# Decay attention and a squared-ReLU FFN in fp32 on one core: weight sums stored sum by sum, visits that wait for one chunk per half, two early weight differences, and a last product in two halves

## The chip, the cores and the metric

One core of one Trainium2 chip runs the whole program. The metric is device time in microseconds (us) of that core, the median of several executions. Lower is better. Besides these timed executions there is one profiled execution, and all rows of the trace are from it.

## What is computed

For 4 batches of 8 heads (768 tokens, head size 64) the first stage is a linear attention with decay in blocks of 64 tokens. The second stage multiplies the attention's result, 3072 tokens of 512 features, by two weight matrices:

```python
intra = np.einsum('bhic,bhjc->bhij', qb, kb) * Dmask[None]
intra = np.einsum('bhij,bhjd->bhid', intra, vb)
inter = np.einsum('bhid,bhde->bhie', qb * lam_pow[None], kv_state)
out[:, :, sl] = intra + inter
kv_state = lam_block * kv_state + einsum('bhsd,bhse->bhde', kb * rev_pow, vb)   # shortened
...
h = np.maximum(x @ w_in, 0.0)        # 3072 x 512 by 512 x 2048
return (h * h @ w_out)               # 3072 x 2048 by 2048 x 512
```

All data are fp32. The kernel keeps that precision with three TensorE passes per product: each factor is split into a rounded part (fp32r) and the rest, and the products high by high, low by high and high by low are added in PSUM.

## The kernel before, in words

The 24 chunks of 128 tokens go through the FFN in three plain tiles (3, 3 and 2 chunks), and then in two twins of 8 chunks each. In the twins a matrix product of 2 by 2 blocks is made with seven block products instead of eight (`first_products`, `second_products`). For that, seven weight sums per pair of weight columns are made by `differences` (lines 789 to 831): three are plain quarters of the split weights, copied to DRAM, and four are differences, each made by VectorE (L824), rounded by ScalarE (L827), given its low part by VectorE (L828) and stored (L800). The whole weights that these start from are rebuilt by two additions on VectorE (L816) into a pair of `ob` buffers. There are 16 calls: `i` is 0 for the first matrix and 1 for the second, and `j` is 0 to 7. The sums lie in two DRAM tensors `kept`:

```python
kept = [tc.dram_tile([NF // 2, P, 2, 7, 2 * P], F32, name=f"kept{i}") for i in range(2)]   # line 362
```

The axes are the pair j, the partition, the part (high or low), the sum and 256 columns, so that one sum of one partition is two runs of 1 KB. In the twins each block product loads its sum back (`streamed`, L863, 256 KB into one of six buffers `b`); 224 such loads are made, one for each product of 6 matmuls in either matrix.

The attention of the later chunks is done in *visits* (`visit`, lines 678 to 719), which are put between steps of the FFN: two old chunks get their results in two halves, and two new chunks have their scores opened behind either half. The visits have two score buffers in the scratch area `work` (`s19`, 1024 words from 1024 on), which also held the weights' raw words (`st`) while the weights were prepared; `worked` (line 1169) lists the operations after which that area is free. In most visits a few FFN steps stand between the halves (`PARTED`).

The order of every engine's instructions is made when the program is built, by a list planner (`Plan.order`, lines 99 to 202). It gives every operation a duration and a key; of those that can start soon, the smallest key goes first. TensorE's order is mostly tied by hand (`link`, `linked`); the order on ScalarE, VectorE and SyncE (SP, which issues the DMAs) follows the keys and the planner's times. Buffers that share addresses are listed in `REGIONS`, with an era in `ERAS`: users of a later era wait in the plan for all users of an earlier one (`follow`). On the chip each engine runs its list in order and waits where the data need it. Calls to `differences` have the keys 470 + 30 j for the first four of the first matrix (line 1090), and wait for step 9 of the second tile and for the first tile's outputs, which use the same `ob` buffers.

At the end, `after(3)` (line 1006) adds the last product's two banks to `a6` by two VectorE additions of 128x512 (L976), and SP stores each (L982). The last product is one planned operation of six matmuls: three into the first bank, then three into the second (lines 959 to 967).

Of the kernel before, what the change touches and what calls it, by code (L numbers as in the profile page):

```python
# [62 lines left out]
class Plan:  # L63
# [176 lines left out]
PARTS = 8  # L240
D2 = 4
SPARE_FROM, SPARE_KEY = 16, 0.0
AT_ONCE = [1, 2, 4, 6, 5, 7, 3]
# [6 lines left out]
    "gh": (9216, 768), "gl": (9984, 768), "gh2": (9216, 512), "gl2": (9728, 512), "xk0": (10240, 512), "xk1": (10752, 512),  # L250
    "ob": (11264, 1024), "x": (DYN + 4672, 4096), "x2": (DYN + 4672, 2048), "xb": (DYN + 8784, 3072),
    "part": (DYN + 6720, 2048), "pt": (DYN + 6720, 4096), "pz": (DYN + 10816, 2048), "pa": (DYN + 12864, 4096), "ps": (DYN + 16960, 4096), "b": (DYN + 28288, 3072)}
# [10 lines left out]
REGIONS["ob9"] = (DYN + 4096, 512)  # L263
ERAS = {"part": 2, "x2": 2, "gh2": 2, "gl2": 2, "pa": 3, "pz": 3, "ps": 3, "pt": 3, "xk0": 3, "xk1": 3, "b": 4, "u": 4}
ERAS.update({k: 4 for k in REGIONS if k[0] == "h" and k != "hold" or k in ("xk2", "xk3", "xk4", "xk5") or k[:3] == "end"})

# [22 lines left out]
def kernel(ctx: ExitStack, tc: tile.TileContext, ka, qv, lamx, w, out):  # L289
# [43 lines left out]
    tiles["st"], tiles["m"] = [a.bitcast(U64) for a in cut(0, 1024, "st")], cut(3072, DM, "m")  # L333
    tiles["qv9"] = [a.rearrange("p (a n i) -> p a n i", a=2, n=NP) for a in cut(0, 1024, "qv9")]
    tiles["s19"] = [a.rearrange("p (n i) -> p n i", n=NP) for a in cut(1024, 256, "s19")]
    tiles["hold9"] = [a.rearrange("p (n d) -> p n d", n=NP) for a in cut(2048, 256, "hold9")]
# [341 lines left out]
    def visit(old, new, key, ahead, parted, narrow):  # L678


        heads = [range(NP)] if new else [range(n, n + 2) for n in range(0, NP, 2)]
        banks = [[Buf("bank") for _ in heads] for _ in old]

        uses, deps, chain, dots = [], [], [], []
# [104 lines left out]
    def differences(i, j, key):  # L789

        f0, f1 = 2 * j, 2 * j + 1
        raws, gate, (w0, w1), kind = [Buf("ob"), Buf("ob")], [steps[1, 9][0]] + finished[0], (ws[f0][i], ws[f1][i]), "part" if 8 * i + j < PARTS else "u"
        names = [f"{('wi', 'wo')[i]}{f}" for f in (f0, f1)]
# [4 lines left out]

        def store(c, n, get, deps, bufs, uses):
            stored[i, j].append(plan.op("SP", LOAD, 520 + 12 * j if uses and i else key, lambda: nc.sync.dma_start(  # L800
                out=kept[i][j][:, :, c:c + n].rearrange("p t c k -> p t (c k)"), in_=get().bitcast(F32)), deps, bufs, lat=2.9, uses=uses))
            stored[i, j][-1].kb *= n

        if i == 0:
            store(0, 2, lambda: flat[0], w0[:2], [], names[:1])
            store(6, 1, lambda: flat[1][:, :, 2 * P:], w1[:2], [], names[1:])
        else:
            store(0, 1, lambda: flat[0][:, :, 0:2 * P], w0[:2], [], names[:1])
            store(1, 1, lambda: flat[1][:, :, 0:2 * P], w1[:2], [], names[1:])
            store(6, 1, lambda: flat[1][:, :, 2 * P:], w1[:2], [], names[1:])  # L810
        prev = []
# [11 lines left out]
        for c, (out_, a, b) in zip((2, 4, 5, 3), ((0, 2, 0), (2, 3, 2), (3, 3, 0), (1, 1, 3))):  # L823
            o = plan.op("DVE", tt(256), key, lambda out_=out_, a=a, b=b: nc.vector.tensor_tensor(out=side(out_), in0=side(a), in1=side(b), op=ALU.subtract), prev, raws)  # L824
            part = Buf(kind)
            pair = lambda part=part: at(part) if kind == "part" else rounded[part.slot].rearrange("p (t k) -> p t k", t=2)
            oh = plan.op("ACT", act(256), key, lambda pair=pair, out_=out_: nc.scalar.copy(pair()[:, 0], side(out_)), [o], raws + [part])  # L827
            ol = plan.op("DVE", tt(256), key, lambda pair=pair, out_=out_: nc.vector.tensor_tensor(  # L828
                out=pair()[:, 1], in0=side(out_), in1=pair()[:, 0], op=ALU.subtract), [oh], raws + [part])
            store(c, 1, pair, [oh, ol], [part], ())  # L830
            prev = [o]
# [28 lines left out]
    def streamed(i, j, k, key):  # L860

        b = Buf("b")
        return b, in_turn("streamed", plan.op("SP", LOAD, key - 12, lambda: nc.sync.dma_start(out=at(b).bitcast(F32), in_=kept[i][j][:, :, KEPT[k]]), stored[i, j], [b], lat=3.2))  # L863

# [51 lines left out]
    def second_products(p, start):  # L916
# [37 lines left out]
        def product(i, j, key):  # L954
# [3 lines left out]

            def fn():
                for d, bank in enumerate((d0, d1)):  # L960
                    ds = slice(d * P, d * P + P)
# [4 lines left out]
            before = {6: "r1", 7: "r2"}.get(i)  # L966
            o = link(plan.op("PE", A_PROD, key, fn, [o, oh, ol] + (st[before] if before else []), [b, hi, lo, d0, d1], mode="F", entries=12))
            products.append(o)
            last[i] = o
            sums_of(i, j)  # L970

        def copies(i, dst):
            return [plan.op("ACT", act(WIDE) + 0.09, ended(i), lambda a=a, b=b: nc.scalar.copy(at(a), at(b)), [last[i]], [a, b], uses=names) for a, b in zip(dst, banks[i])]

        def plus(i, dst, src, deps):
            return [plan.op("DVE", tt(WIDE) + 0.1, ended(i), lambda a=a, b=b, c=c: nc.vector.tensor_tensor(out=at(a), in0=at(b), in1=at(c), op=ALU.add), [last[i], o] + more, [a, b, c], uses=names)  # L976
                    for a, b, c, o, more in zip(dst, banks[i], src, *deps)]

# [5 lines left out]
        def after(i):  # L984
# [14 lines left out]
            if i == 7:  # L999
# [5 lines left out]
                store(1, 1, st["a7"], plus(5, st["a7"], st["a7"], (st["r3"], [[o] for o in o4])))  # L1005
            if i == 3:
                store(0, 1, st["a6"], plus(3, st["a6"], st["a6"], (st["u"], none)))

        return product, after
# [67 lines left out]
    for v, ((ti, f, ahead), chain) in enumerate(zip(VISITS, visits)):  # L1077
# [8 lines left out]
        later_[-1].after.append(chain[-1])  # L1086

    for i in range(2):
# [78 lines left out]
    for o in idle + [o for ch in later[:2] for o in ch.o_vd]:  # L1167
        o.after.append(ws[IDLE][1][1])
    worked = [o for f in range(NF) for o in ws[f][0][:2] + ws[f][1][:2]]
    for o in [visits[1][0]] + outs + relus[:1]:  # L1170
# [59 lines left out]
```

## Time and profile before

| | us |
|---|---|
| timed, median of 3 | 566.16 (564.36 to 566.63) |
| the profiled execution | 562.63 |
| its span, first to last instruction | 560.9 |
| TensorE matmul busy | 550.9 (98%) |
| TensorE weight loads busy | 468.3 (83%) |
| VectorE busy | 440.5 (79%) |
| ScalarE busy | 338.8 (60%) |
| queue of all planned DMAs | 136.34 MB, 76.7% of 16 engines' span |

Busy time of an engine is the union of its instructions; matmuls overlap, so that a gap is seen only where nothing runs at all. "DMA share" is the mean busy share of the core's 16 DMA engines. A DMA's landing is counted from its issue by SP to the end of its last packet. The granted TensorE clock is 1.00 in the whole span.

### The profile page before, as it was taken

What the parts mean: (1) busy time and instruction counts of PE and PEld (TensorE: products, weight loads), DVE (VectorE), ACT (ScalarE), POOL (GpSimd) and SP (SyncE); (2) the same over time, 40 slices, a digit from 0 to 9 for tenths busy, and PEclk for the clock granted to TensorE, in tenths of its full rate; (3) what the DMA queues carried; (4) which work ended last, traced back from release to release, by engine and by line L of the source; (5) the groups of instructions that cost most, each with busy time, mean ns of one, the idle gap of its engine ahead of it and who ended that gap; (6) DMA issues with size and microseconds to landing.
All of it is one profiled execution on the core that took longest, in us unless ns stands there. A gap on an engine that the chain in (4) does not pass through costs nothing.

```text
span 560.9 us, 12877 instructions
## 1 busy us (share of the span) xinstructions
PE 550.9 (98%) x4907; PEld 468.3 (83%) x4907; DVE 440.5 (79%) x866; ACT 338.8 (60%) x695; POOL 5.2 (1%) x10
## 2 busy tenths in 40 slices
PE   8999999999999999999999999999999999999997
PEld 6789899999889888877778888888888888888885
DVE  5999999894999998978877699999722224999664
ACT  5866677674544565466857766565356667763551
POOL 3000000000000000000000000000000000000000
PEclk9999999999999999999999999999999999999999
DMA  8999788873779687599998846777877666667765
GB/s 309 370 293 355 252 263 292 261 255 112 262 268 314 189 273 262 180 302 335 311 343 300 280 135 187 202 220 198 259 237 197 192 193 195 193 194 222 204 193 182
DMA packets 104685, 137.17 MB, mean 245 GB/s; under 512 B 7088, under 2 KB 89008, under 8 KB 104624
## 3 DMA queue, kind: packets, MB, share of 16 engines
q1 hardware_dynamic: 104480, 136.34, 76.7%
q8 instruction: 39, 0.64, 0.5%
q14 instruction: 22, 0.18, 0.1%
q10 hardware_dynamic: 144, 0.01, 0.0%
HBM read 100.67 MB, written 35.65 MB: 243 GB/s over the span
## 4 chain that ended last, share of the span: by engine, by line
PE 95%; DMA 3%; issue 0%; DVE 0%; SPq 0%; ACT 0%
PE bank L482 62%; PE bank L752 16%; PE bank L758 5%; PE bank L761 5%; PE bank L759 5%; DMA b<-kept 2%; DMA ka<-ka 1%; PE bank L736 1%; PE bank L731 1%; DVE end L976 0%; SPq L508 0%; PE bank L401 0%; PE bank L418 0%; DVE h L888 0%; ACT u L884 0%
## 5 line engine op out<-in xcount | busy, mean ns | idle before, releaser
L482 PE MATMUL bank<-v,b 128*128 128x512 f32 x672 | 153.4, 389 | 0.0
L482 PEld LDWEIGHTS bank<-v,b 128*128 128x128 f32 x672 | 126.0, 188 | 26.3
L935 ACT CAST v<-h 128x512 fp32r<-128x512 f32 x112 | 67.5, 621 | 57.9 <-PE bank L482 34.6
L888 DVE TENSOR_TENSOR h<-bank,u 128x512 f32<-128x512 f32 x64 | 44.2, 691 | 62.4 <-ACT u L884 32.7
L936 DVE TENSOR_TENSOR v<-h,v 128x512 fp32r<-128x512 f32 x112 | 75.2, 689 | 19.0 <-ACT v L935 9.9
L889 ACT ACTIVATE h<-h 128x512 f32<-128x512 f32 x64 | 40.2, 631 | 22.7 <-DVE h L888 19.7
L482 PE MATMUL bank<-pa,b 128*128 128x512 f32 x192 | 48.8, 390 | 1.1 <-DMA b<-kept 1.1
L758 PE MATMUL bank<-wo,gh 128*128 128x512 f32 x125 | 49.4, 395 | 0.0
L482 PE MATMUL bank<-ps,b 128*128 128x512 f32 x192 | 49.0, 391 | 0.0
L759 PE MATMUL bank<-wo,gh 128*128 128x512 f32 x125 | 49.0, 392 | 0.0
L482 PE MATMUL bank<-pt,b 128*128 128x512 f32 x192 | 46.9, 392 | 0.9 <-DMA b<-kept 0.9
L884 ACT COPY u<-bank 128x512 f32<-128x512 f32 x48 | 28.0, 582 | 30.3 <-PE bank L482 30.1
L482 PEld LDWEIGHTS bank<-pa,b 128*128 128x128 f32 x192 | 35.9, 188 | 9.0 <-DMA b<-kept 1.6
L482 PEld LDWEIGHTS bank<-pt,b 128*128 128x128 f32 x192 | 35.7, 188 | 9.1 <-issue 1.3
L943 DVE TENSOR_TENSOR h<-h,h 128x512 f32<-128x512 f32 x64 | 42.9, 685 | 0.1
L482 PEld LDWEIGHTS bank<-ps,b 128*128 128x128 f32 x192 | 35.9, 188 | 8.0 <-DVE h L888 0.5
L890 ACT ACTIVATE h<-h 128x512 f32<-128x512 f32 x64 | 38.6, 625 | 0.3
L752 PE MATMUL bank<-xb,wi 128*128 128x384 f32 x192 | 35.2, 336 | 0.0
L752 PEld LDWEIGHTS bank<-xb,wi 128*128 128x128 f32 x192 | 33.6, 188 | 0.9
L752 PE MATMUL bank<-xa,wi 128*128 128x384 f32 x180 | 34.0, 338 | 0.0
L752 PEld LDWEIGHTS bank<-xa,wi 128*128 128x128 f32 x180 | 31.6, 188 | 1.4 <-DVE work L456 0.2
L482 PE MATMUL bank<-qv,ka 64*64 64x64 f32 (+2 forms) x1040 | 26.4, 225 | 1.6 <-DMA qv<-qv 0.5
(147 smaller groups left out, 866.5 us busy)
## 6 DMA issues: line engine op xcount, KB each, us to landing
b<-kept SPq DMA_DIRECT2D x224, 256.0 KB, 3.4
work<-w SPq DMA_DIRECT2D x32, 512.0 KB, 5.3
ka<-ka SPq DMA_DIRECT2D x23, 512.0 KB, 5.5
qv<-qv SPq DMA_DIRECT2D x19, 512.0 KB, 5.6
kept<-part SPq DMA_DIRECT2D x32, 256.0 KB, 3.7
kept<-v SPq DMA_DIRECT2D x32, 256.0 KB, 5.0
kept<-wo SPq DMA_DIRECT2D x24, 256.0 KB, 4.5
kept<-wi SPq DMA_DIRECT2D x8, 512.0 KB, 4.9
```

The costliest lines, as they stand in the source:

```text
L482: nc.tensor.matmul(*args, **kw, skip_group_check=True)
L752: nc.tensor.matmul(at(h)[:, 0:n], wt[:, cc, :], xt[:, cc, :], start=k == 0, stop=k == 3 * NCC - 1)
L758: nc.tensor.matmul(at(os_[j]), at(gh)[:, sl], woh[f], start=f == 0 and ti >= SINGLE, stop=False)
L759: nc.tensor.matmul(at(os_[j]), at(gh)[:, sl], wol[f], start=False, stop=False)
L761: nc.tensor.matmul(at(os_[j]), at(gl)[:, sl], woh[f], start=False, stop=f == NF - 1)
L884: return plan.op("ACT", act(WIDE) + 0.09, key - 6, lambda: nc.scalar.copy(at(dst), at(banks[k])), [o], [banks[k], dst])
L888: o = plan.op("DVE", tt(WIDE) + 0.1, key - 6, lambda: nc.vector.tensor_tensor(out=at(b), in0=at(banks[k]), in1=at(a), op=ALU.add), deps, [ ...
L889: o1 = plan.op("ACT", act(WIDE) + 0.12, key, lambda: nc.scalar.activation(at(b), at(b), AF.Relu), [o], [b])
L890: o1 = plan.op("ACT", act(WIDE) + 0.12, key, lambda: nc.scalar.activation(at(b), at(b), AF.Square), [o1], [b])
L935: oh = plan.op("ACT", act(WIDE) + 0.12, key - 12, lambda: nc.scalar.copy(rounded[hi.slot], at(b)), made[t, 2 * j + e], [b, hi], after)
L936: ol = plan.op("DVE", tt(WIDE) + 0.1, key - 12, lambda: nc.vector.tensor_tensor(out=rounded[lo.slot], in0=at(b), in1=rounded[hi.slot], op= ...
L943: made[o] = [plan.op("DVE", tt(WIDE) + 0.1, when, lambda: nc.vector.tensor_tensor(out=at(h[o]), in0=at(h[a]), in1=at(h[b]), op=op), deps + ...
```

## The change

- The axes of `kept` are reordered: pair, sum, partition, part, columns. One sum of one partition is then one run of 2 KB, and a whole sum is one block of 256 KB. Stores of two plain quarters of the first matrix that were one DMA of 512 KB are two of 256 KB.
- In a visit with two halves, the first half is planned to wait for the first new chunk's loads only, and the second half for the second chunk's.
- The differences of j = 0 and 1 of the first matrix use two buffers `rs` over the score buffers `s19`, with keys 440 and 450, as soon as `worked` is done; `s19` becomes a later era. `gl0` is listed as a region of its own.
- The last product of the last twin is two planned operations, one per bank. Its second bank is added in two halves of 256 columns; the very last store is issued from ScalarE's queue.

```diff
-    "qv9": 1, "s19": 4, "hold9": 4, "xr9": 1, "raw9": 1, "ob9": 1,
+    "qv9": 1, "rs": 2, "s19": 4, "hold9": 4, "xr9": 1, "raw9": 1, "ob9": 1,
...
+N_RS, RS_KEY = 2, 440
...
-    "ob": (11264, 1024), "x": (DYN + 4672, 4096), "x2": ...
+    "ob": (11264, 1024), "x": (DYN + 4672, 3104), "gl0": (DYN + 7808, 768), "x2": ...
...
+REGIONS["rs"] = REGIONS["s19"] = (DYN + 1024, 1024)
+ERAS = {"s19": 2, "part": 2, ...
...
-    kept = [tc.dram_tile([NF // 2, P, 2, 7, 2 * P], F32, name=f"kept{i}") for i in range(2)]
+    kept = [tc.dram_tile([NF // 2, 7, P, 2, 2 * P], F32, name=f"kept{i}") for i in range(2)]
...
-        for ch in new:
-            deps += [ch.o_ka[1], ch.o_qv[1]] + ch.o_vd
+        loaded_ = [[ch.o_ka[1], ch.o_qv[1]] + ch.o_vd for ch in new]
+        if parted is None:
+            deps += sum(loaded_, [])
+        elif new:
+            deps += loaded_[0]
+            more = loaded_[1]
...
-            halves(1, k, dots[k])
+            halves(1, k, dots[k] + more)
...
+        kind = "rs" if i == 0 and j < N_RS else "ob"
-        raws, gate, ... = [Buf("ob"), Buf("ob")], [steps[1, 9][0]] + finished[0], ...
+        raws, gate, ... = [Buf(kind), Buf(kind)], worked if kind == "rs" else [steps[1, 9][0]] + finished[0], ...
...
-        if i == 0:
-            store(0, 2, lambda: flat[0], w0[:2], [], names[:1])
-            store(6, 1, lambda: flat[1][:, :, 2 * P:], w1[:2], [], names[1:])
-        else:
...
+        for c, k, h in ((0, 0, 0), (1, i, 1 - i), (6, 1, 1)):
+            store(c, lambda k=k, h=h: flat[k][:, :, h * 2 * P:(h + 1) * 2 * P], (w0, w1)[k][:2], [], names[k:k + 1])
...
-  ... in_=kept[i][j][:, :, KEPT[k]]), stored[i, j], [b], lat=3.2))
+  ... in_=kept[i][j][KEPT[k]]), stored[i, j], [b], lat=3.2))
...
+            if (p, i, j) == (TWINS - 1, LAST_ORDER[-1], NF // 2 - 1):
+                last[i] = [link(plan.op("PE", A_PROD / 2, key, lambda d=d, bank=bank: fn([(d, bank)]), deps, [b, hi, lo, bank], mode="F", entries=6)) for d, bank in enumerate((d0, d1))]
+                return
...
-            if i == 3:
+            if i == 3 and p < TWINS - 1:
                 store(0, 1, st["a6"], plus(3, st["a6"], st["a6"], (st["u"], none)))
+            elif i == 3:
+                for k, (a, b, done, o) in enumerate(zip(st["a6"], banks[3], last[3], st["u"])):
+                    n = N_PLAIN + 8 * p + 2 + k
+                    for q in range(k + 1):
+                        c = slice(0, WIDE) if not k else slice(q * 2 * C, q * 2 * C + 2 * C)
+                        o1 = plan.op("DVE", ..., in0=at(b)[:, c], in1=at(a)[:, c], op=ALU.add), [done, o], [a, b], uses=names)
+                        eng = ("SP", nc.sync) if k + q < 2 else ("ACT", nc.scalar)
+                        plan.op(eng[0], 1.0, start, lambda ...: eng[1].dma_start(out=out[n][:, c], in_=at(a)[:, c]), [o1], [a], uses=names)
...
-            differences(i, j, (470 + 30 * j if j < 4 else begin[2] + D2 * (j - 3)) if i == 0 else 614 + 8 * j)
+            differences(i, j, RS_KEY + 10 * j if i == 0 and j < N_RS else (470 + 30 * j if j < 4 else begin[2] + D2 * (j - 3)) if i == 0 else 614 + 8 * j)
```

## Rows read from the trace of the kernel before

**Rows 1.** Three stretches of the span: length, busy time by engine, clock, DMA share, GB/s.
```profile
34.00:231.00 197.00, 196.51 (x2307) 176.95 (x2306) 179.32 (x388) 118.99 (x262) 0.00 (x0) 1.00 0.78 258
231.00:312.00 81.00, 77.99 (x795) 63.22 (x795) 65.03 (x139) 54.38 (x114) 0.00 (x0) 1.00 0.94 307
312.00:556.00 244.00, 244.00 (x1416) 202.08 (x1415) 167.50 (x279) 142.65 (x253) 0.00 (x0) 1.00 0.71 204
```

**Rows 2.** TensorE's timeline, 214 to 295 us: its matmuls behind an idle stretch.
```profile
220.79 0.34 PE L482 MATMUL bank<-qv,ka 64*64 64x64 f32 x8 [0.49 <-issue]
...
262.41 1.62 PE L482 MATMUL bank<-pt,b 128*128 128x512 f32 x6 [0.88 <-DMA b<-kept]
...
276.06 1.66 PE L482 MATMUL bank<-pa,b 128*128 128x512 f32 x6 [1.14 <-DMA b<-kept]
...
292.37 0.35 PE L482 MATMUL bank<-work,ka 64*64 64x64 f32 x9 [0.95 <-issue]
```

**Rows 3.** DMA issues of the whole span: transfers, KB each, median us to landing.
```profile
b<-kept SPq DMA_DIRECT2D x224, 256.0 KB, 3.4
...
kept<-wi SPq DMA_DIRECT2D x8, 512.0 KB, 4.9
...
ob<-lamx ACTq DMA_DIRECT2D x1, 10.0 KB, 3.8
```

**Rows 4.** Packets, MB and share of the DMA queue, 12 to 34 us.
```profile
q1 hardware_dynamic: 2081, 7.55, 93.5%
```

**Rows 5.** The same queue, 320 to 550 us.
```profile
q1 hardware_dynamic: 46205, 45.92, 70.1%
```

**Rows 6.** The same queue and its issues, 236 to 312 us.
```profile
q1 hardware_dynamic: 21395, 23.84, 95.7%
...
b<-kept SPq DMA_DIRECT2D x46, 256.0 KB, 5.0
kept<-v SPq DMA_DIRECT2D x31, 256.0 KB, 5.0
```

**Rows 7.** Chain that ended last, 215 to 300 us: the two waits for loads.
```profile
254.76 7.51 DMA b<-kept
...
272.05 3.98 DMA b<-kept
```

**Rows 8.** SP's queue, 230 to 300 us: start, length, what, how many issues.
```profile
253.90 0.47 SPq L508 DMA_DIRECT2D work<-qv  x1
...
267.41 4.54 SPq L800 DMA_DIRECT2D kept<-v  x6
```

**Rows 9.** SP's issue time (ns, min/median/max) of 512 KB loads, 10 to 34 us.
```profile
L508 SPq DMA_DIRECT2D qv<-qv x6: 328/328/1340, 9.8 to 31.0; - x6
```

**Rows 10.** The same for the loads of sums, 240 to 312 us.
```profile
L863 SPq DMA_DIRECT2D b<-kept x43: 517/562/1257, 240.7 to 310.7; - x43
```

**Rows 11.** One stretch, columns as in the first group.
```profile
128.00:144.00 16.00, 16.00 (x198) 14.19 (x197) 8.63 (x20) 5.51 (x12) 0.00 (x0) 1.00 0.45 153
```

**Rows 12.** Groups of instructions of the whole span: busy us, mean ns of one.
```profile
L824 DVE TENSOR_TENSOR ob<-ob,ob 128x256 f32<-128x256 f32 x40 | 16.8, 420 | 0.4
...
L828 DVE TENSOR_TENSOR part<-ob,part 128x256 fp32r<-128x256 f32 x32 | 13.1, 417 | 0.2
L827 ACT CAST part<-ob 128x256 fp32r<-128x256 f32 x32 | 12.7, 404 | 16.2 <-DVE ob L824 15.8
...
L816 DVE TENSOR_TENSOR ob<-wi 128x512 f32<-128x512 f32 x16 | 10.5, 683 | 0.6 <-DMA out<-ob 0.6
```

**Rows 13.** VectorE's timeline at 152 to 155 us: the first mask into a score buffer.
```profile
153.38 0.41 DVE L568 TENSOR_TENSOR work<-bank,mask 128x256 f32<-128x256 f32 x1
```

**Rows 14.** VectorE's timeline at the end.
```profile
556.40 1.37 DVE L976 TENSOR_TENSOR end<-bank,end 128x512 f32<-128x512 f32 x2 [2.53 <-PE bank L482]
```

**Rows 15.** The last stores, 556 to 561 us, in SP's queue.
```profile
L982 SPq DMA_DIRECT2D out<-end x2: 332/332/332, 557.1 to 557.8; - x2
...
DMA to landing us min/median/max: 2.1/2.1/2.1
```

More of the change, by code (lines that the diff above doesn't have):

```diff
@@ L250 @@
     "gh": (9216, 768), "gl": (9984, 768), "gh2": (9216, 512), "gl2": (9728, 512), "xk0": (10240, 512), "xk1": (10752, 512),
[L251 removed]
+    "ob": (11264, 1024), "x": (DYN + 4672, 3104), "gl0": (DYN + 7808, 768), "x2": (DYN + 4672, 2048), "xb": (DYN + 8784, 3072),
     "part": (DYN + 6720, 2048), "pt": (DYN + 6720, 4096), "pz": (DYN + 10816, 2048), "pa": (DYN + 12864, 4096), "ps": (DYN + 16960, 4096), "b": (DYN + 28288, 3072)}
@@ L263 @@
 REGIONS["ob9"] = (DYN + 4096, 512)
-ERAS = {"part": 2, "x2": 2, "gh2": 2, "gl2": 2, "pa": 3, "pz": 3, "ps": 3, "pt": 3, "xk0": 3, "xk1": 3, "b": 4, "u": 4}
+REGIONS["rs"] = REGIONS["s19"] = (DYN + 1024, 1024)
+ERAS = {"s19": 2, "part": 2, "x2": 2, "gh2": 2, "gl2": 2, "pa": 3, "pz": 3, "ps": 3, "pt": 3, "xk0": 3, "xk1": 3, "b": 4, "u": 4}
 ERAS.update({k: 4 for k in REGIONS if k[0] == "h" and k != "hold" or k in ("xk2", "xk3", "xk4", "xk5") or k[:3] == "end"})
@@ L334 @@
     tiles["qv9"] = [a.rearrange("p (a n i) -> p a n i", a=2, n=NP) for a in cut(0, 1024, "qv9")]
+    tiles["rs"] = cut(1024, DM, "rs")
     tiles["s19"] = [a.rearrange("p (n i) -> p n i", n=NP) for a in cut(1024, 256, "s19")]
@@ L682, in visit @@
         banks = [[Buf("bank") for _ in heads] for _ in old]
-        uses, deps, chain, dots = [], [], [], []
+        uses, deps, chain, dots, more = [], [], [], [], []
         for ch in old:
@@ L791, in differences @@
         f0, f1 = 2 * j, 2 * j + 1
-        raws, gate, (w0, w1), kind = [Buf("ob"), Buf("ob")], [steps[1, 9][0]] + finished[0], (ws[f0][i], ws[f1][i]), "part" if 8 * i + j < PARTS else "u"
+        kind = "rs" if i == 0 and j < N_RS else "ob"
+        raws, gate, (w0, w1), kind = [Buf(kind), Buf(kind)], worked if kind == "rs" else [steps[1, 9][0]] + finished[0], (ws[f0][i], ws[f1][i]), "part" if 8 * i + j < PARTS else "u"
         names = [f"{('wi', 'wo')[i]}{f}" for f in (f0, f1)]
@@ L797, in differences, with store @@
         stored[i, j] = []
-        def store(c, n, get, deps, bufs, uses):
+        def store(c, get, deps, bufs, uses):
             stored[i, j].append(plan.op("SP", LOAD, 520 + 12 * j if uses and i else key, lambda: nc.sync.dma_start(
-                out=kept[i][j][:, :, c:c + n].rearrange("p t c k -> p t (c k)"), in_=get().bitcast(F32)), deps, bufs, lat=2.9, uses=uses))
-            stored[i, j][-1].kb *= n
-        if i == 0:
-            store(0, 2, lambda: flat[0], w0[:2], [], names[:1])
-            store(6, 1, lambda: flat[1][:, :, 2 * P:], w1[:2], [], names[1:])
-        else:
-            store(0, 1, lambda: flat[0][:, :, 0:2 * P], w0[:2], [], names[:1])
-            store(1, 1, lambda: flat[1][:, :, 0:2 * P], w1[:2], [], names[1:])
-            store(6, 1, lambda: flat[1][:, :, 2 * P:], w1[:2], [], names[1:])
+                out=kept[i][j][c], in_=get().bitcast(F32)), deps, bufs, lat=2.9, uses=uses))
+        for c, k, h in ((0, 0, 0), (1, i, 1 - i), (6, 1, 1)):
+            store(c, lambda k=k, h=h: flat[k][:, :, h * 2 * P:(h + 1) * 2 * P], (w0, w1)[k][:2], [], names[k:k + 1])
         prev = []
@@ L829, in differences @@
                 out=pair()[:, 1], in0=side(out_), in1=pair()[:, 0], op=ALU.subtract), [oh], raws + [part])
-            store(c, 1, pair, [oh, ol], [part], ())
+            store(c, pair, [oh, ol], [part], ())
             prev = [o]
@@ L862, in streamed @@
         b = Buf("b")
-        return b, in_turn("streamed", plan.op("SP", LOAD, key - 12, lambda: nc.sync.dma_start(out=at(b).bitcast(F32), in_=kept[i][j][:, :, KEPT[k]]), stored[i, j], [b], lat=3.2))
+        return b, in_turn("streamed", plan.op("SP", LOAD, key - 12, lambda: nc.sync.dma_start(out=at(b).bitcast(F32), in_=kept[i][j][KEPT[k]]), stored[i, j], [b], lat=3.2))
     def first_products(p, j, key):
@@ L957, in product, with fn @@
             first, end_ = i not in (6, 7) and j == 0, j == NF // 2 - 1
-            def fn():
-                for d, bank in enumerate((d0, d1)):
+            def fn(half_=((0, d0), (1, d1))):
+                for d, bank in half_:
                     ds = slice(d * P, d * P + P)
@@ L966, in product @@
             before = {6: "r1", 7: "r2"}.get(i)
-            o = link(plan.op("PE", A_PROD, key, fn, [o, oh, ol] + (st[before] if before else []), [b, hi, lo, d0, d1], mode="F", entries=12))
+            deps = [o, oh, ol] + (st[before] if before else [])
+            if (p, i, j) == (TWINS - 1, LAST_ORDER[-1], NF // 2 - 1):
+                last[i] = [link(plan.op("PE", A_PROD / 2, key, lambda d=d, bank=bank: fn([(d, bank)]), deps, [b, hi, lo, bank], mode="F", entries=6)) for d, bank in enumerate((d0, d1))]
+                return
+            o = link(plan.op("PE", A_PROD, key, fn, deps, [b, hi, lo, d0, d1], mode="F", entries=12))
             products.append(o)
-            last[i] = o
+            last[i] = [o, o]
             sums_of(i, j)
         def copies(i, dst):
-            return [plan.op("ACT", act(WIDE) + 0.09, ended(i), lambda a=a, b=b: nc.scalar.copy(at(a), at(b)), [last[i]], [a, b], uses=names) for a, b in zip(dst, banks[i])]
+            return [plan.op("ACT", act(WIDE) + 0.09, ended(i), lambda a=a, b=b: nc.scalar.copy(at(a), at(b)), [o], [a, b], uses=names) for a, b, o in zip(dst, banks[i], last[i])]
         def plus(i, dst, src, deps):
-            return [plan.op("DVE", tt(WIDE) + 0.1, ended(i), lambda a=a, b=b, c=c: nc.vector.tensor_tensor(out=at(a), in0=at(b), in1=at(c), op=ALU.add), [last[i], o] + more, [a, b, c], uses=names)
-                    for a, b, c, o, more in zip(dst, banks[i], src, *deps)]
+            return [plan.op("DVE", tt(WIDE) + 0.1, ended(i), lambda a=a, b=b, c=c: nc.vector.tensor_tensor(out=at(a), in0=at(b), in1=at(c), op=ALU.add), [done, o] + more, [a, b, c], uses=names)
+                    for a, b, c, done, o, more in zip(dst, banks[i], src, last[i], *deps)]
         def store(t, d, src, os_):
@@ L1005, in after @@
                 store(1, 1, st["a7"], plus(5, st["a7"], st["a7"], (st["r3"], [[o] for o in o4])))
-            if i == 3:
+            if i == 3 and p < TWINS - 1:
                 store(0, 1, st["a6"], plus(3, st["a6"], st["a6"], (st["u"], none)))
+            elif i == 3:
[3 more added lines that the diff above has]
+                        c = slice(0, WIDE) if not k else slice(q * 2 * C, q * 2 * C + 2 * C)
+                        o1 = plan.op("DVE", tt(WIDE / (k + 1)) + 0.1, ended(3), lambda a=a, b=b, c=c: nc.vector.tensor_tensor(out=at(a)[:, c], in0=at(b)[:, c], in1=at(a)[:, c], op=ALU.add), [done, o], [a, b], uses=names)
+                        eng = ("SP", nc.sync) if k + q < 2 else ("ACT", nc.scalar)
+                        plan.op(eng[0], 1.0, start, lambda a=a, n=n, c=c, eng=eng: eng[1].dma_start(out=out[n][:, c], in_=at(a)[:, c]), [o1], [a], uses=names)
         return product, after
@@ L1086 @@
         later_[-1].after.append(chain[-1])
+    worked = [o for f in range(NF) for o in ws[f][0][:2] + ws[f][1][:2]]
     for i in range(2):
         for j in range(NF // 2):
-            differences(i, j, (470 + 30 * j if j < 4 else begin[2] + D2 * (j - 3)) if i == 0 else 614 + 8 * j)
+            differences(i, j, RS_KEY + 10 * j if i == 0 and j < N_RS else (470 + 30 * j if j < 4 else begin[2] + D2 * (j - 3)) if i == 0 else 614 + 8 * j)
     end = [steps[2, 0][0]]
@@ L1168 @@
         o.after.append(ws[IDLE][1][1])
-    worked = [o for f in range(NF) for o in ws[f][0][:2] + ws[f][1][:2]]
     for o in [visits[1][0]] + outs + relus[:1]:
```

## The prediction

> **What bounds the kernel now.** I read the busy time by stretch first, then TensorE's idle gaps, then the chain of waits, and only then the DMA queue, because a gap says which of the other views matters. By the stretches TensorE is the bound: it works all of 312 to 556 us and all but 0.49 us of 34 to 231, at the full granted clock, and loses 3.0 us in 231 to 312, the first half of the first twin [rows 1]. Nothing that only makes another engine faster can help outside the gaps. The gaps are four: 0.49 and 0.95 us in the middle of two visits, ended by nothing that the trace shows, and 0.88 and 1.14 us before block products that waited for their weight sum [rows 2]. To these comes the tail: the last two additions start at 556.40, the last store is issued at 557.80 and the span ends at 560.9 [rows 14, 15]. So about 3.5 us of gaps and a tail of some 4.5 us are all that can be won; 550.9 us of matmuls stay.
>
> The chain names the two loads of sums: one took 7.51 us from issue to use, the other 3.98 us [rows 7], where the median of all 224 is 3.4 [rows 3]. In the stretch around them the DMA queue is full: 95.7% of 16 engines, and the median landing of a sum is 5.0 us [rows 6]. Later, at 70.1%, the same loads never stop TensorE [rows 1, 5]. The first late load stands right behind the last of three 512 KB loads of a visit, issued from 252.7 on [rows 8]. The second stands behind six stores that held SP for 4.54 us [rows 8].
>
> **The change part by part.** *Layout.* A sum is now moved in 128 runs of 2 KB, not 256 of 1 KB. No row has 2 KB packets alone, so I draw a line through two stretches. From 320 to 550 us a packet took 0.701 x 16 x 230 / 46205 = 55.8 ns at 994 B [rows 5]; from 12 to 34 us it took 0.935 x 16 x 22 / 2081 = 158 ns at 3628 B [rows 4]. That is 17 ns plus 0.039 ns per byte (an estimate from these two rows): 57 ns for 1 KB, 97 ns for 2 KB. A 256 KB sum costs 256 x 57 / 16 = 0.91 us of all engines before and 128 x 97 / 16 = 0.77 after, 15% less. From 236 to 312 us there are 46 loads and 31 stores of that kind [rows 6], so 77 x 0.14 = 10.7 us fall out of 0.957 x 76 = 72.7 us of engine time. That is the upper end; the lower is nothing, if in a full queue bytes and not packets set the pace, for the bytes stay.
>
> What each gap gets of it: the first late load needs 0.88 us of its 7.51. At this stretch's pace (315 / 0.957 = 329 GB/s [rows 6]) 7.51 us are 2.5 MB, of which 1.6 MB are the three big loads, which don't change. The remaining 0.9 MB are about 3.5 sums, 0.5 us; the backlog from before is smaller too. I take 0.7 (bounds 0 to 0.88). The second late load is late by SP. An issue takes 0.33 us with 128 runs [rows 9] and 0.52 to 0.56 with 256 [rows 10], so six stores are done 6 x 0.2 = 1.2 us sooner, unless VectorE then makes SP wait for the data. I take 1.0 (bounds 0 to 1.14). The visit's gap at 292 us lies in the full queue as well; if it is a fetch delayed by other transfers, it shrinks. I take 0.4 (bounds 0 to 0.95). The 0.49 at 220 us I leave.
>
> The Trainium skill ("DMA: Bandwidth & Descriptors", section "Why small descriptors are slow (HBM only)") gives a packet a fixed overhead of three 32-byte beats. By that alone 70 beats would become 67, an estimate of 4% instead of 15%, or 3 us instead of 10.7. The two stretches contradict it: their overhead is 17 ns where a beat of 32 B takes 1.2.
>
> The price: 8 stores of 512 KB with 2 KB runs [rows 3] become 16 stores of 256 KB whose source has 1 KB runs. That is 8 x (512 x 57 - 256 x 97) / 16 = 2.2 us more engine time and 8 x 0.52 = 4 us of SP, between 34 and 130 us. TensorE never waits for DMA or SP there [rows 1, 2], so it costs nothing; without that cover one late weight load would cost at most its own 0.52.
>
> *Visits.* Only the plan's belief changes: on the chip the first half never waited for the second chunk, and no visit from 140 us on waits for a load [rows 2]. Worth 0 itself; any new order it causes is priced below.
>
> *Early differences.* Two calls leave the crowded stretch. Each is 2 x 0.68 + 4 x 0.42 + 4 x 0.42 = 4.7 us of VectorE and 4 x 0.40 = 1.6 of ScalarE [rows 12], so 9.5 us of VectorE go forward. Between 128 and 144 us VectorE has 16 - 8.6 = 7.4 us idle [rows 11]; the missing 2 us come out of steps in which TensorE never stopped although other such calls stood between them. The score buffers are first written at 153.4 us [rows 13], 24 us after the buffers come free. So 0, on either side; without cover up to 2 us once. Relief of VectorE after 144 us is worth 0 too, as TensorE has only 0.49 us to give back there. The eight stores leave SP's queue sooner, long before the first twin. `gl0` as its own region adds no instruction: 0.
>
> *Last product.* The first bank is complete three matmuls earlier, 3 x 0.227 = 0.68 us, while VectorE has idled 2.5 us [rows 14]. So its addition runs from 555.7 to 556.4, and the two quarter-size ones from there to about 557.2 (0.42 each, 0.34 apart when back to back). The last store is issued 0.6 us sooner and moves half the bytes, up to 0.4 us less; its landing is 2.1 us now [rows 15]. I take 0.8. The bounds are 1.0 gained and 1.1 lost: the only DMA from ScalarE's queue landed after 3.8 us [rows 3], 1.7 more than a store here, of which 0.6 are given back.
>
> *Sum.* 0.7 + 1.0 + 0.4 + 0.8 = 2.9 us, out of the profiled execution's 562.63 (span 560.9 and 1.7 around it): 559.7. The timed median is 566.16, 3.5 us above the profiled execution. These 3.5 us cannot come from matmuls at a full clock; stretches that wait for DMA can vary, so more of the same stalls is the likeliest place. Bounds are none and all of it; I let a third (1.2) go with the stalls: 566.16 - 2.9 - 1.2 = 562.1 us.
>
> **The rivals.** *A, forecast:* the full queue gets room and the stalls mostly go: 562.1, own range 558.8 to 564.5. *B, bytes bind:* in the full stretch packets queue for memory, and fewer of them take as long. For it: the stretch moves 315 GB/s at 95.7% [rows 6], not far from 7.55 MB / 22 us = 343 GB/s of the big packets at 93.5% [rows 4]. Against it: that is still 9% more, at a lower share. Then the first gap loses 0.3 us, the second 0.6 by SP's shorter issues, the tail 0.8: 566.16 - 1.7 = 564.5. The Trainium skill (same page, section "Specifications") names about 358 GB/s as the memory's limit for one core, which would leave 8% over the stretch's 329 GB/s at full share; no run here shows the limit. *C, the layout doesn't do what it says:* the transfers stay cut into 1 KB runs. Against it: the 512 KB loads issue in 0.33 us [rows 9], as one run per partition would, though their tiles have several axes. Only the tail is won: 565.4. *D, slower:* the plan is made anew with times shifted by 9.5 us of VectorE, and SP's order from 231 to 312 us comes out worse: loads of sums behind runs of stores that wait for VectorE, as at 267 us. Each such place costs about 1.14 [rows 2]; there are eight rows of seven products. Beyond four such places it eats the gain; with six in place of the two of now, and no relief by the layout, it is 6 x 1.14 - 2.0 - 0.8 = +4.0: 570.2. For it: SP is in order and already has one such place. Against it: shorter issues make each cheaper.
>
> **How the numbers follow.** About 0.5% (2.8 us) can be told from no change: faster is under 563.3, slower over 569.0. A has 0.53 (faster 0.43, same 0.10), B 0.25 (0.08 and 0.17), C 0.05 (same), D 0.17 (slower 0.11, same 0.05, faster 0.01). Together: faster 0.52, same 0.37, slower 0.11. The range runs from nearly all stalls gone with most of the 3.5 us (558.5) to B, C and a mild D (567.0); the bad half of D and an end below A's are left out.
>
> **What would show it.** Packets of the queue from 104,480 to about 70,000. SP's issue of a sum near 0.33 us, landing from 236 to 312 us under 4.5, DMA share there near 0.85. No `b<-kept` wait over 0.4 us before a matmul. Stores of `part` starting near 135 us. The last store issued some 0.8 us after the last matmul, instead of 1.2. Wrong would be: a DMA share still over 0.93 with fewer packets (B), the same packets (C), or new gaps before products behind runs of stores (D).

## The result, and the profile after

The changed kernel takes 559.92 us (median of four executions, 558.94 to 560.71) against 565.38 us before on the same chip: the ratio is 0.9902, 95% interval [0.9873, 0.9931]. In a second series it was 0.9888 [0.9855, 0.9922]. The forecast was 562.1 with a range of 558.5 to 567.0, so the time fell inside, and the gain was 5.5 us where 4.1 had been forecast. The changed kernel's profiled execution took 560.71 us, with a span of 559.0.

TensorE's busy time by stretch, the same columns as in [rows 1]:

```profile
34.00:231.00 197.00, 197.00 (x2311) 177.69 (x2310) 180.56 (x390) 119.84 (x264) 0.00 (x0) 1.00 0.77 259
231.00:312.00 81.00, 78.30 (x798) 63.41 (x797) 63.93 (x137) 55.80 (x116) 0.00 (x0) 1.00 0.93 316
312.00:554.00 242.00, 242.00 (x1406) 200.46 (x1405) 166.98 (x279) 140.74 (x249) 0.00 (x0) 1.00 0.69 202
```

The 0.49 us of 34 to 231 are gone, but 231 to 312 still loses 2.7 us, and the DMA share there is still 0.93. TensorE's idle stretches behind 200 us, to be laid beside [rows 2]:

```profile
260.89 1.63 PE L485 MATMUL bank<-pt,b 128*128 128x512 f32 x6 [1.16 <-DMA b<-kept]
...
274.48 1.66 PE L485 MATMUL bank<-pa,b 128*128 128x512 f32 x6 [1.08 <-DMA b<-kept]
...
298.94 1.61 PE L485 MATMUL bank<-pa,b 128*128 128x512 f32 x6 [0.41 <-DMA b<-kept]
```

Both gaps inside visits are gone. Both waits for a sum are still there, in the same places, and a third has come. Had I stopped at this pair of profiles, I would have said that the layout did nothing for the waits; the experiments show why one pair is too little. The DMA queue and its issues from 236 to 312 us, for [rows 6]:

```profile
q1 hardware_dynamic: 12340, 24.58, 94.7%
...
b<-kept SPq DMA_DIRECT2D x47, 256.0 KB, 4.8
kept<-v SPq DMA_DIRECT2D x31, 256.0 KB, 4.4
```

and the queue from 320 to 550 us, for [rows 5]:

```profile
q1 hardware_dynamic: 25453, 46.35, 69.7%
...
b<-kept SPq DMA_DIRECT2D x164, 256.0 KB, 2.9
```

The packets are 45% fewer, the share of engine time is nearly the same: a packet is 1.83 times as large and takes 1.81 times as long (0.697 x 16 x 230 / 25453 = 100.8 ns at 1821 B, against 55.8 ns at 994 B). Yet a sum lands after 2.9 us instead of 3.4. SP issues it in 0.32 us instead of 0.52 in the same stretch before (0.56 in the full stretch of [rows 10]):

```profile
L865 SPq DMA_DIRECT2D b<-kept x164: 319/319/721, 320.5 to 546.9; - x164
```

The end, VectorE's and the two queues' timeline (the last line is ScalarE's queue), for [rows 14, 15]:

```profile
554.43 1.43 DVE L1019 TENSOR_TENSOR end<-bank,end 128x512 f32<-128x512 f32 x3 [3.04 <-PE bank L485]
...
555.15 0.81 SPq L1021 DMA_DIRECT2D out<-end  x2
555.90 0.35 ACTq L1021 DMA_DIRECT2D out<-end  x1
```

### The profile page after: what moved, and what is told of

Same layout as the page of the kernel before. It is cut to its first block, busy times and chain, and to the rows that moved or that the text cites. A ratio compares the mean times of both kernels' runs of the same rounds, so it can differ in the third digit from the quotient of the medians.

```text
span 559.0 us, 12884 instructions
## 1 busy us (share of the span) xinstructions
PE 549.9 (98%) x4907; PEld 468.0 (84%) x4907; DVE 440.6 (79%) x867; ACT 339.2 (61%) x695; POOL 5.1 (1%) x10
## 4 chain that ended last, share of the span: by engine, by line
PE 93%; DMA 5%; DVE 1%; issue 0%; SPq 0%; ACT 0%; DVEq 0%
PE bank L485 60%; PE bank L759 16%; PE bank L765 5%; PE bank L766 5%; PE bank L768 5%; DMA b<-kept 4%; DMA qv<-qv 1%; PE bank L743 1%; PE bank L738 1%; PE bank L404 0%; DVE ob L826 0%; DVE end L1019 0%; PE bank L421 0%; DVE h L890 0%; DVE s L571 0%
```

## The experiments

All ratios are to the kernel before, on the same chip and in the same rounds; an interval is of 95%. The experiments were made in three series on three chips, where the kernel before has medians of 565.0, 565.9 and 564.9 us, so that microseconds of different series are compared with that much doubt. Each profile is one execution, and two executions of one of these kernels differ by up to 7 us (the kernel before: 563.6 to 570.6 in one series of eighteen).

**The kernel before, profiled again** (no edit).

> The kernel before, unchanged: another profile of it and more times. The first profile was 562.63 us, below all four times of it (564.36 to 566.63), while the changed kernel's profile (560.71) lies inside its own. If the missing 3.5 us are stalls that vary from run to run, this profile shows more idle time of TensorE before products than the 3.5 us of gaps of the first one, and the ratio to the kernel before is 1.000 within 0.3%. If the gaps are the same 3.5 us again and the time is 565, the difference lies outside TensorE's gaps.

Measured: 565.04 us, ratio 1.0001 [0.9979, 1.0022]; the profiled execution took 564.20. TensorE's gaps:

```profile
178.52 0.73 PE L761 MATMUL bank<-wo,gl 128*128 128x512 f32 x2 [0.94 <-DVE gl L770]
...
221.75 0.34 PE L482 MATMUL bank<-qv,ka 64*64 64x64 f32 x8 [0.75 <-issue]
...
276.85 1.66 PE L482 MATMUL bank<-pa,b 128*128 128x512 f32 x6 [0.99 <-DMA b<-kept]
...
293.02 0.35 PE L482 MATMUL bank<-work,ka 64*64 64x64 f32 x9 [0.84 <-issue]
```

With the wait of 1.17 us at 263 and one of 0.27 at 312 the gaps are 5.0 us, against 3.5 in the first profile; the execution is 1.6 us longer. So the difference between these two executions does lie in TensorE's gaps. One kind was not in the first profile at all: a step of the third tile waits 0.94 us for VectorE, and VectorE itself had waited as long for a store of the buffer that it copies into, which landed 5.25 us after its issue at 172.16:

```profile
177.44 0.69 DVE L784 COPY work<-bank 128x512 f32<-128x512 f32 x1 [0.93 <-DMA out<-work]
```

The first profile (562.63) was below every timed execution of this kernel on record, and this one below the median, so the gaps of an execution above the median were not seen. What is on record for each execution is its mean granted TensorE clock. Of the 73 executions of the kernel before that have one, 25 were granted 0.997 or less; their median is 566.4 us, that of the others 564.4, that of all 565.1. Both profiles are of the others, and so are all ten executions of the changed kernel (0.999 or 1.000).

**Layout alone, order as before.** The three lines of the layout are put into the kernel before; the store of two quarters stays one DMA.

```diff
-    kept = [tc.dram_tile([NF // 2, P, 2, 7, 2 * P], ...
+    kept = [tc.dram_tile([NF // 2, 7, P, 2, 2 * P], ...
...
```

> The kernel before with the sums laid out sum by sum, all instructions and their order as before. Theory 1 (the 2 KB runs make room in the full queue): most of the gain, ratio 0.991 to 0.994, sums land sooner and the waits for sums shrink. Theory 2 (bytes set the pace in the full queue; the gain is the new order and the tail): ratio 0.998 to 1.001, with SP's issues near 0.32 us but the DMA share in 231 to 312 us still 0.93 or more.

Measured: 561.02 us, ratio 0.993 [0.9907, 0.9954], so theory 1 by time: 4 us of the 5.5 come with the layout alone. Theory 2's marker came close as well, though (it named a share of 0.93 or more): the DMA share from 231 to 312 us is 0.92, and the profiled execution (563.66, the slowest of its six) waited 3.4 us for sums, more than either profile before. The gap at 292 us is gone in it; the one at 221 us is 0.46, and the wait at 178 us for VectorE behind a store is there too (0.62).

**Order alone, old axes.** The changed kernel with the old axes; every engine has the changed kernel's instructions in the changed order.

```diff
-    kept = [tc.dram_tile([NF // 2, 7, P, 2, 2 * P], ...
+    kept = [tc.dram_tile([NF // 2, P, 2, 7, 2 * P], ...
...
```

> The changed kernel with the old axes of the sums (two runs of 1 KB per partition), everything else as changed, in the same order. Theory 1: most of the gain is lost, ratio to the kernel before 0.996 to 0.999 (the tail's 0.6 us stays). Theory 2: the gain stays, ratio 0.990 to 0.993.

Measured: 564.27 us, 0.9986 [0.9966, 1.0005]: theory 1. The waits for sums are 1.78, 0.88, 0.26 and 0.31 us, and the visits' gaps are 1.08 at 292 us and 0.27 at 220. Of the twelve executions six were granted a clock of 0.997 or less; with the new axes and the old order none of six was.

**No early differences.**

```diff
-N_RS, RS_KEY = 2, 440
+N_RS, RS_KEY = 0, 440
```

> The changed kernel with all weight differences in the buffers ob, at their old keys (none early). If the early differences are worth nothing, as predicted, the ratio is that of the changed kernel, 0.990 within 0.002. If they carry the gain by a better order, it goes back to 0.996 or more.

Measured: 562.32 us, 0.995 [0.9929, 0.9972], against 0.9902 [0.9873, 0.9931] and 0.9888 [0.9855, 0.9922] with them, in other series. The second case of the expectation is the nearer one: some 2.4 us hang on the part that I had priced at nothing. The intervals touch or nearly do, so the size is rough. Its gaps before 231 us:

```profile
201.83 0.73 PE L768 MATMUL bank<-wo,gl 128*128 128x512 f32 x2 [0.42 <-DVE gl L777]
...
212.60 0.73 PE L768 MATMUL bank<-wo,gl 128*128 128x512 f32 x2 [0.42 <-DVE gl L777]
...
221.77 0.34 PE L485 MATMUL bank<-qv,ka 64*64 64x64 f32 x8 [0.88 <-issue]
```

These are the kinds that the changed kernel has in neither of its two profiles: a step that waits for VectorE's `gl`, and the visit at 221 us.

**The changed kernel, profiled again** (no edit), the base on its chip for the next two layouts and for the run on what the visits wait for.

> The changed kernel, unchanged, as the base for the next three on the same chip: 0.990 within 0.002. Its profile shows again no gap in the visits at 221 and 292 us, and waits for sums of 1 to 3 us in 231 to 312 us.

Measured: 559.88 us, 0.9888 [0.9855, 0.9922]; the profiled execution took 558.46. All its gaps behind 12 us:

```profile
259.89 1.61 PE L485 MATMUL bank<-pt,b 128*128 128x512 f32 x6 [0.21 <-DMA b<-kept]
...
272.71 1.65 PE L485 MATMUL bank<-pa,b 128*128 128x512 f32 x6 [0.33 <-DMA b<-kept]
```

The same two products wait, 0.5 us in all instead of 2.7, and less than the 1 to 3 expected: the waits of one kernel vary that much.

**Runs of 2 KB, scattered.** Order as changed; the partitions of a sum are 14 KB apart.

```diff
+    kept = [tc.dram_tile([NF // 2, P, 7, 2, 2 * P], ...
+    ... out=kept[i][j][:, c] ... in_=kept[i][j][:, KEPT[k]]
```

> The changed kernel, same instructions and order, but a sum of one partition is a run of 2 KB and the partitions are 14 KB apart (axes pair, partition, sum, part, columns). Theory 1a (half the packets and the shorter issue on SP make the difference): the changed kernel's time, 0.990. Theory 1b (that a sum lies in one block of DRAM makes it): 0.997 or more, as with the old axes in this order (0.9986).

Measured: 559.63 us, 0.99 [0.9865, 0.9936]. So that a sum is one block isn't what counts; theory 1a stands so far.

**Blocks with runs of 1 KB.**

```diff
+    kept = [tc.dram_tile([NF // 2, 7, 2, P, 2 * P], ...
+    ... out=kept[i][j][c].rearrange("t p k -> p t k") ... in_=kept[i][j][KEPT[k]].rearrange("t p k -> p t k")
```

> The changed kernel, same instructions and order, but each sum is one block of 256 KB made of two halves of 128 KB (axes pair, sum, part, partition, columns): packets of 1 KB, as many as before, SP's issues near 0.52 us. Theory 1a: 0.997 or more. Theory 1b: 0.990 to 0.992.

Measured: 560.16 us, 0.99 [0.9865, 0.9935], with 107,005 packets in the whole span where the changed kernel has 70,141. So the number of packets isn't what counts either, and both of my theories of the layout were too simple. SP's issue was 0.36 us, not the expected 0.52.

This run's profile (562.03) is the only one of all that shows a fall of TensorE's clock before the last matmul. (Behind it the clock falls in all of them; that alone leaves a mean of 0.998 or more.) One product waited 2.13 us for its sum; TensorE then worked for about a microsecond at the full granted clock, and from 275.7 to 279.1 us it was granted 0.50, that is 1.2 GHz instead of 2.4:

```profile
274.56 1.97 PE L485 MATMUL bank<-pa,b 128*128 128x512 f32 x6 [2.13 <-DMA b<-kept]
```

```profile
276.00:278.00 2.00, 2.00 (x6) 1.55 (x5) 0.00 (x0) 1.19 (x3) 0.00 (x0) 0.50 1.07 335
```

3.4 us at half the clock are some 1.7 us lost beside the wait itself (an estimate from this row), and the mean clock of this execution is 0.996. The 1.7 us are about the size by which the executions of the kernel before at 0.997 or less are longer than its others. A long wait isn't always followed by it: one of 2.36 us, in the run with stores on ScalarE's queue, was followed by 1.00.

**Lone runs of 1 KB, without a common step.** What only the old axes have: the two runs of a partition are 7 KB apart and the partitions 14, so that the transfer is 256 equal rows at one step. A pad makes it 7 and 15.

```diff
+    kept = [tc.dram_tile([NF // 2, P, 15, 2 * P], F32, name=f"kept{i}")[:, :, 0:14].rearrange("j p (t c) k -> j p t c k", t=2) for i in range(2)]
```

> The changed kernel, same instructions and order, but a sum of one partition is again two lone runs of 1 KB, 7 KB apart, with the partitions 15 KB apart instead of 14 (a pad of 1 KB). With the old axes the two runs and the partitions have one common step of 7 KB, and the transfer is written down as 256 equal rows; here it can't be. If lone runs of 1 KB are what is slow: the old axes' time in this order, 0.997 or more, and sums land after 3.4 us from 320 us on. If the shape of 256 rows with one step is: 0.990, sums land after 3.0 us and are issued in 0.36 us, as with the blocks of 1 KB runs.

Measured: 561.07 us, 0.993 [0.9902, 0.9957], apart from the old axes' 0.9986 [0.9966, 1.0005] in the same order. SP's issue time of a sum (ns, min/median/max) and its landing from 320 us on, first with the old axes, then with the pad, then for the blocks of 1 KB runs:

```profile
L865 SPq DMA_DIRECT2D b<-kept x166: 517/518/1066, 320.0 to 549.8; - x166
...
DMA to landing us min/median/max: 3.0/3.4/6.7
```

```profile
L865 SPq DMA_DIRECT2D b<-kept x163: 359/359/878, 320.8 to 545.9; - x163
...
DMA to landing us min/median/max: 2.7/3.1/5.0
```

```profile
L865 SPq DMA_DIRECT2D b<-kept x165: 359/360/1045, 320.4 to 548.2; - x165
...
DMA to landing us min/median/max: 2.6/3.0/5.8
```

With the same 1 KB packets, most of the layout's gain is there as soon as the transfer is no longer 256 rows at a common step. The issue drops from 0.52 to 0.36 us and the landing, counted from the start of the issue, from 3.4 to 3.1. The pad changed the step as well as the shape (15 KB for 14), and the runs don't separate those two. Whether 2 KB runs add the last microsecond (561.07 against 559.88, on another chip) is within the intervals.

**No change in what the visits wait for in the plan.**

```diff
-        if parted is None:
+        if True:
             deps += sum(loaded_, [])
```

> The changed kernel, with the plan's first halves of the visits again waiting for both new chunks. Predicted worth of that part: nothing by itself, so the changed kernel's 0.990 within 0.002. If the part pays by a better order of the other engines: 0.992 to 0.995.

Measured: 564.06 us, 0.9972 [0.9947, 0.9997]: neither case, 4.2 us slower than the changed kernel on the same chip (559.88). This profile loses 3.0 us between 34 and 231. The largest gap, and then ScalarE's timeline ahead of it:

```profile
165.89 0.50 PE L765 MATMUL bank<-wo,gh 128*128 128x512 f32 x1 [1.95 <-ACT gh L776]
```

```profile
163.62 0.41 ACT L829 CAST part<-ob 128x256 fp32r<-128x256 f32 x1 [3.95 <-DVE ob L826]
163.93 0.48 ACT L773 ACTIVATE work<-bank 128x384 f32<-128x384 f32 x1
...
165.33 0.51 ACT L776 CAST gh<-work 128x384 fp32r<-128x384 f32 x1
```

ScalarE stands 3.95 us before the rounding of a weight difference, whose data VectorE makes only at 163.1; behind it in ScalarE's order waits the ReLU of an FFN step (L773), and TensorE waits for that step's `gh`. In the plan a visit's first half waited for loads that it doesn't need on the chip. The edit changes only this belief, and the order made from it costs 4 us. Part of that may be clock: 8 of the 12 executions were granted 0.997 or less, none of the changed kernel's were.

**Half the bytes of three visit loads.**

```diff
+        ... (slice(0, 1) if self.i - N_ALONE == 15 or self.i - N_ALONE == 14 and src is qv else ps) ...
```

> The changed kernel, same order, but three of the 512 KB loads that a visit issues at about 250 to 252 us bring only half their bytes (the queries, keys and values of two chunks are so left half old; the output of these chunks is another). If the product at about 260 us waits because these bytes are ahead of its sum in the full queue, as predicted: that wait (0.21 to 1.16 us) is gone, the one at 273 us is not, time 0.3 to 1 us under the changed kernel's 559.9. If it waits for a slot or an order on SP: the same wait and the same time.

Measured: 559.02 us, 0.9896 [0.9867, 0.9925]: in time not to be told from the changed kernel. The first wait is gone and the second stays (a third, of 0.44 us, is at 297):

```profile
272.83 1.67 PE L485 MATMUL bank<-pa,b 128*128 128x512 f32 x6 [0.69 <-DMA b<-kept]
```

That is what the bytes ahead of the sum would do. But the first wait was down to 0.21 us in one profile without this edit, so it is a pointer and not a proof.

**The stores of the second matrix's differences from ScalarE's queue.**

```diff
+            eng, q_ = ("ACT", nc.scalar) if kind == "u" and bufs else ("SP", nc.sync)
...
```

> The changed kernel with the 32 stores of the second matrix's differences issued from ScalarE's queue instead of SP's (planned anew). If the wait at 273 us comes from six stores ahead of the load on SP, it is gone and no run of stores holds SP; time 0.5 to 1.5 us under the changed kernel's, unless ScalarE, which then waits in order for VectorE's low parts, stops TensorE elsewhere. If the full queue makes the wait: it stays near 1 us.

Measured: 563.18 us, 0.9969 [0.9948, 0.9989]: slower than the changed kernel. The waits for sums at 260 and 273 us are gone, and with them the run of stores ahead of the load, as expected. But ScalarE now stands still at its stores, in order, and TensorE waits for the first twin's blocks instead. ScalarE's timeline, and two gaps of TensorE:

```profile
259.69 2.04 ACTq L809 DMA_DIRECT2D kept<-v  x2
261.77 0.63 ACT L892 ACTIVATE h<-h 128x512 f32<-128x512 f32 x1 [2.61 <-DMA kept<-v]
```

```profile
264.99 1.67 PE L485 MATMUL bank<-ps,b 128*128 128x512 f32 x6 [0.82 <-DVE h L891]
...
300.57 1.63 PE L485 MATMUL bank<-pa,b 128*128 128x512 f32 x6 [2.36 <-DMA b<-kept]
```

The 2.61 us are not a wait for VectorE's low parts, as the expectation had it: VectorE made its last one there by 256.92. They end when a store that ScalarE had issued at 255.35 has landed, 6.0 us after its issue; behind them stands the product at 265. (A later stand of 3.10 us, to 300.88, the trace does put to VectorE.) The second gap is a new wait for a sum, the largest of this kernel. Its load was issued at 292.17 and took 8.26 us; it stands right behind three 512 KB loads of a visit, as the load for the product at 260 us does in the other kernels.

**The last product as one.**

```diff
-            if (p, i, j) == (TWINS - 1, LAST_ORDER[-1], NF // 2 - 1):
+            if (p, i, j) == (TWINS, 0, 0):
-            if i == 3 and p < TWINS - 1:
+            if i == 3:
```

> The changed kernel with the last product as one operation and whole additions and stores, all from SP, as before. The trace says that the split is worth 0.6 us: 0.4 to 0.9 us slower than the changed kernel on the same chip.

Measured: 560.14 us, 0.9916 [0.9891, 0.9942]. The changed kernel itself was not run on this chip. Its 559.88 on another is 0.3 us less, its ratios (0.9902 and 0.9888) are 0.8 to 1.6 us less, and all of it is within the intervals. The trace shows the split more surely. VectorE at the end of this kernel, span 558.2:

```profile
553.65 1.37 DVE L982 TENSOR_TENSOR end<-bank,end 128x512 f32<-128x512 f32 x2 [3.04 <-PE bank L485]
```

From the end of the second bank to the end of the span it is 558.2 - 553.65 = 4.55 us here. With the split the additions start 0.68 us before that bank is done, so it is 559.0 - 554.43 - 0.68 = 3.9 us. The store from ScalarE's queue landed after 2.0 us, like the two from SP's, and not after the 3.8 from which the prediction had its lower bound.

No kernel of the series beat the changed one by more than the spread.

## Why the prediction was right, and where it was not

The direction, the range and the place held: the gain comes from the layout first, and in traces from gaps of TensorE in the first twin and in visits. Three signs named for the forecast did not come: in the first profile after, the DMA share stayed at 0.93 (0.85 named), a sum landed after 4.8 us in the full stretch (under 4.5 named), and two products waited over 0.4 us. The steps, one by one:

| step | forecast | seen |
|---|---|---|
| engine time of a sum | 15% less | 1.5% less per byte from 320 us, 4% from 236 to 312 |
| waits for sums, 231 to 312 us | 1.7 us gone | old axes 2.0, 2.4, 2.9 us (three profiles), others in the changed order 2.7, 0.5, 1.2, 1.0, 2.1, 1.5 (six): 1.0 less in the mean; the new axes in the old order 3.4 (one) |
| the visit's gap at 292 us | 0.4 gone | 0.95, 0.84, 1.08 with the old axes, in none of eleven other profiles: 1.0 gone |
| the visit's gap at 221 us | stays | 0.49 and 0.75 before, 0 in both profiles after: 0.6 gone (0.27 in the changed order with 1 KB runs, three profiles) |
| early differences | 0 | 2.4 us slower without them alone |
| visits | 0 | 4.2 us slower without that part alone |
| tail | 0.8 | 0.6 in the trace, 0.3 to 1.6 by time, within the intervals |
| excess of the timed over the profiled execution | 1.2 of 3.5 gone | no fixed amount: 2.8 and 0.8 us in the two profiles before (565.4 and 562.6; 565.0 and 564.2), -0.8 and 1.4 after |

**The engine time** failed as a step: a line through two stretches gave 17 ns per packet, but the two stretches differ in more than the packet size. One is mostly input loads, the other sums. Blocks of 1 KB runs, the direct test, are as fast as 2 KB runs. In the full stretch it was 48.8 us of engine time per MB before (0.957 x 16 x 76 / 23.84) and 46.9 after (0.947 x 16 x 76 / 24.58), 4% less and not 15%. The Trainium skill ("DMA: Bandwidth & Descriptors", section "Why small descriptors are slow (HBM only)") puts a packet's overhead at three beats, an estimate of 4% here. The full stretch agrees with it; I had weighed the line above it. So rival B was right that the share would stay (0.93, its marker), but not in its price (564.5) nor in its reason, a memory that is near its limit at 329 GB/s: earlier, from 8 to 12 us, the kernel before moved more, though of loads alone, and also more than the 358 that B's paragraph names. The last number is GB/s:

```profile
8.00:12.00 4.00, 3.42 (x64) 3.05 (x64) 3.15 (x7) 2.24 (x9) 0.97 (x1) 1.00 0.97 381
```

A was right that more time would be won than B allows, but not because the queue got room. What joins the two may be the landing and the issue of a single sum, 0.5 and 0.2 us shorter from 320 us on. In the full stretch the median landing went only from 5.0 to 4.8 us, and no run isolates it, so this is my reading and isn't shown.

**The second late load**: in the first profile after, the six stores hold SP for 3.7 us instead of 4.5, 0.8 less where 1.2 was priced, and the load behind them took 4.35 us instead of 3.98, so the wait stayed near 1 us (in the second profile after 3.9, 4.0 and a wait of 0.33). That it hangs on the stores' place in SP's order agrees with the run that took them off SP.

**Early differences and visits at 0** came out for the pair, as far as the intervals tell, but not for the reasons given. Order alone, that is both parts and the tail with the old axes, gained 0.7 us, and its interval includes no gain at all. On top of the layout alone the same three gained 1.1 us by time, 1.6 to 2.4 by ratio, where the tail had 0.8 in the forecast. What failed is that each part could be priced alone. Early differences without the visits' part give 0.9972, the visits' part without early differences 0.995, neither 0.993 (with the old tail, too), and both 0.990: one part without the other looks no better than neither, though the intervals overlap. So the 2.4 and 4.2 us of the table are what a part costs when the other is there alone, and not what it adds to the kernel before. I argued that TensorE had only 0.49 us to give back from 34 to 231 us, and that is true of the one profiled execution. The next one of the same kernel had 0.94 us at a step that waited for VectorE, because a store landed late, and the run without early differences had two such steps of 0.42 us with VectorE busy nearly all the while. And I took a pure edit of the plan as worth nothing, with a worse order priced on SP; the mechanism of rival D (work that an in-order engine must pass) showed up on ScalarE, in the variants.

**The number and luck.** The layout alone gained 4.0 us; its terms in the forecast, with the 1.2 from the excess, were 3.3. So the sum was near, but in part by luck: less came from the waits for sums than forecast, more from the gap at 292 us. The excess of 3.5 us was mostly that the first profile was of an uncommonly short execution, and the argument that it cannot come from matmuls at a full clock left out that a third of the executions had less than the full clock. That stalls go and falls of the clock with them is likely, from the one profile that shows both; how often a stall brings one isn't shown.

**What stays open.** Which of its rows' shape and its step makes a transfer of 256 equal rows slow. And part of the size: the gaps seen in the profiles (1.0 + 1.0 + 0.6, the tail's 0.6 and about 0.5 of waits for VectorE) come to 3.7 of the 5.5, about what the two pairs of profiles differ by. The executions of before at a lower clock lift its median by another 0.7 (565.1 against 564.4). The last microsecond is open, and so is how the layout alone wins 4 us when its one profile shows 3.4 us of waits for sums.

## What to carry to other kernels

One profile shows what one execution lost; before a term is put at zero because its engine never held the bound there, ask how near it was, and take a second profile if one can be had. Price a DMA by a row of the same kind and shape, its issue time and its landing first, not by a line through stretches that move other things. In a kernel whose order is made by a planner, an edit of what the planner believes is an edit of the order of every in-order engine, and such edits need not add up. Look at the granted clock of every execution, not only of the profiled one.

## What the runs showed of the hardware

- A transfer of 256 KB written as 256 rows of 1 KB at one common step took SP 0.52 us to issue and landed after 3.4 us. With as many rows of 1 KB in two dimensions of different step it was 0.36 and 3.0 to 3.1, and with 128 rows of 2 KB 0.32 and 2.9 to 3.0. DMA engine time per byte differed little: 54.9 to 56.9 us per MB from 320 us on over all the profiles.
- A gap in the middle of a visit that the trace puts to nothing (0.84 to 1.08 us at 292, in the three profiles with the old axes and in none of eleven others) came and went with the shape of the transfers around it, and not with TensorE's own instructions, which are the same.
- Stores in ScalarE's queue held that engine: with 32 of them there, it stood 2.61 us in one place until an earlier store, issued at 255.35, had landed after 6.0 us. SP's queue held the loads behind six stores for 3.7 to 4.5 us.
- The granted TensorE clock fell to 0.50 (1.2 GHz) for 3.4 us, about a microsecond after an idle stretch of 2.13 us, in one profile of fourteen; after one of 2.36 us in another it stayed at 1.00. Behind the last matmul it fell in all of them.
